# Moving the even heads' outer-key products behind the fourth unit's dense group in a sliding-window attention kernel

## The chip, the cores and the metric

The kernel runs on one core of one Trainium2 chip. The metric is the device time of one execution in microseconds, the median of several runs. A core has five instruction streams that run side by side and wait for one another through semaphores: TensorE (PE; its weight loads are listed apart as PEld), VectorE (DVE), ScalarE (ACT), GpSimd (POOL) and SyncE (SP), which issues the DMAs here. Each stream executes its instructions in the order in which the program lists them, so an instruction that waits holds up everything behind it on its engine.

## The reference

One block of a transformer with conditioned normalization (adaLN): sliding-window attention (32 heads of 16, window 256 over 2048 tokens, 512 features), then a token-mixing MLP (2048 tokens to 1792 and back). Cut to what matters:

```python
def _A_ref(x, wqkv, wo):                      # B, S, D = 1, 2048, 512; H, Dh, W = 32, 16, 256
    q, k, v = ...                             # from x @ wqkv, per head
    scores = jnp.einsum('bhqd,bhkd->bhqk', q, k) * Dh ** (-0.5)
    mask = (idx[:, None] - idx[None, :] >= 0) & (idx[:, None] - idx[None, :] < W)
    p = _softmax(jnp.where(mask[None, None], scores, -1000000000.0), axis=-1)
    o = jnp.einsum('bhqk,bhkd->bhqd', p, v)
    return (lambda x, *d: x.transpose(*d))(o, 0, 2, 1, 3).reshape(B, S, D) @ wo

def _B_ref(x, w1, b1, w2, b2):
    h = _layernorm(x, axis=-1)
    u = _gelu(jnp.einsum('bsd,sf->bdf', h, w1) + b1)
    return (lambda x, *d: x.transpose(*d))(jnp.einsum('bdf,fs->bds', u, w2) + b2, 0, 2, 1)

mod = (_silu(c) @ w_mod).reshape(c.shape[0], 6, 1, -1)      # sa, ca, ga, sb, cb, gb
h = _layernorm(x, axis=-1) * (1 + ca) + sa
x = x + ga * _A_ref(h, A_wqkv, A_wo)
h = _layernorm(x, axis=-1) * (1 + cb) + sb
return x + gb * _B_ref(h, B_w1, B_b1, B_w2, B_b2)
```

## The kernel before

**Tiling of the attention.** The 2048 tokens are four *token groups* (`tg`) of four blocks of 128. The 32 heads are four groups of eight (`g8`), and of the eight, four are even and four odd; the four of one parity sit on the four 32-row strips of TensorE. One *set* is one `tg` with one `g8`: sixteen sets. A set has five *units* `k` (KINDS, L413):

- k = 0 and k = 1: the even heads against the nearer keys, in two parts;
- k = 2: the *outer* keys (the own block's and the far block's half blocks) for even and odd heads together;
- k = 3 and k = 4: the odd heads against the nearer keys.

In the first token group, sets after the first have four units, since k = 0 takes both parities and k = 3 falls away.

For each unit, `emit_scores` (L579) makes the scores in PSUM tiles `pss` (three buffers, two to a unit), `emit_exp` (L646) has ScalarE turn them into `et` with two exponentials of 128x1024 (L659), and the *products* with the values go into the PSUM tile `po`, which has **one** buffer (L417). `av_a` (L664, matmuls on L673) makes a unit's products for the nearer keys; `av_c` (L680, 32 matmuls on L687) those of the outer keys for one parity, with the rearranged values `Vc`. Unit 2's `av_c` completes the even heads, unit 4's `av_a` and `av_c` the odd ones. When a parity is complete, `norm_out` (L716) has VectorE transpose `po` into one half of `t2` (L719); the next parity's products wait for that. After the odd half, `norm_rest` (L724) goes on: the reciprocal `zr` on VectorE (L730), the quotient `merge` on GpSimd (L731), and the transpose into `OTd` on VectorE (L739).

**Dense groups.** Beside the attention's own work, nearly every unit has one *dense group*, sixteen matmuls on L288 into the PSUM tile `dn`, which also has **one** buffer (L418): projections of queries, keys and values (`qk_group` L316, `v_group` L293) for coming sets, the output projection of the token group before (`wo_group` L382), or parts of the MLP's first matmul (`part_group` L806). In two places it is eight transposes (`transpose_group`, L270). VectorE evacuates each group (L304, L330, L333, L397, L822, L278). `plan` (L828) says which group goes to which unit of a token group, `ul` = 5 `g8` + `k`.

**The order.** It is written out by hand (`manual_schedule`). The loop over the units (L977) emits for unit `u`: the first exponential; the scores of unit `u + 1`; then, if `closes` (L997) holds, the products of unit `u - 1`; the dense group; the second exponential; the dense group's evacuation; and, if `closes` does not hold, the products of unit `u - 1` (L1024). `closes` holds where unit `u - 1` completes a parity, that is, where the present unit is k = 3 (after the outer unit 2) or the next set's k = 0 (after unit 4).

```python
            closes = u > 0 and units[u - 1][2] in (2, 4) and u != 3
            if closes:
                products(u - 1)
            group = at.get(ul)
```

**The planner.** The small steps of VectorE (LayerNorm statistics, scalings, `zr`, `OTd`) stand in `chains`, and `fill` (L789) emits them where a hand-kept clock of the engines (`clock`) says that VectorE has room until a given time. `products` (L949) and the loop add estimated costs to this clock and call `fill`, so what stands where in VectorE's queue, and in GpSimd's behind it, hangs on the order of these calls. `ln23` (L742) is the second LayerNorm of a block: statistics (L747, L749), variance and power on GpSimd (L208, L212), VectorE's scaling into `h2` (L759), two products on GpSimd (L763, L764), statistics again, then L208, L212, `shift` (L218) and the final scaling into `hb` (L219) on GpSimd.

**After the attention.** From L1096 on, TensorE runs the MLP's first matmul (L1080) over the blocks `hb` that are ready, with the output projection of the last four blocks in between (`t_wo`, L1099, matmuls on L1102 into `pa`), which needs all four `OTd` of the last token group, the last set's last. Then follow the rest of the first matmul (L1166), GELU (L1091) and the second matmul (L1202). SP loads `w1b` (L1062) and `w2r` (L1064) meanwhile.

Of the kernel before, what the change touches and what calls it, by code (L numbers as in the profile page):

```python
# [30 lines left out]
def kernel(  # L31
# [261 lines left out]
    def v_group(tg, tl, pool, name="dn"):  # L293
        def mms(parts=range(ND), pv=None):
            pv = pv or pool.tile([P, D], DT.float32, name=name)
            for dc in parts:
                dense(
                    pv, lhsT=h1T[tg][:, dc, tl * P : (tl + 1) * P],
                    rhs=wqkv[:, dc, 2 * D : 3 * D], start=(dc == 0), stop=(dc == ND - 1),
                )  # L300
            return pv

        def evac(pv):
            nc.vector.tensor_copy(out=VaugT[tg][:, tl, :, 0:DH], in_=pv[:].rearrange("p (h d) -> p h d", d=DH))  # L304
            if tl > 1:
                nc.vector.tensor_copy(out=Vc[0][0:64, tl, 0:8, :], in_=VaugT[tg][0:64, tl, 0:8, :])
        return mms, evac, 0.9 if tl > 1 else 0.7
# [107 lines left out]
    with tc.manual_schedule():  # L415
# [136 lines left out]
        def k_piece(lo, hi):  # L552
            nc.scalar.activation(out=KT[0][0][:, lo:hi], in_=pk[:, lo:hi], func=ACT.Copy)
# [10 lines left out]
        def both(tg, g8, k):  # L564

            return tg == 0 and g8 > 0 and k == 0

        units = [
            (tg, g8, k) for tg in range(NG) for g8 in range(ND) for k in range(5) if not (both(tg, g8, 0) and k == 3)
        ]  # L570
# [75 lines left out]
        def emit_exp(u, a):  # L646
            tg, g8, k = units[u]
            kind, par, i = KINDS[k]
            n = 512
            if (tg, kind, i) == (0, "A", 0) and not both(tg, g8, k):  # L650

                n = 256
                if a == 0:
                    state["et"] = epool.tile([P, 2, 4 * P], DT.bfloat16, name="et")
                et = state["et"][:, a, :].rearrange("p (h q) -> p h q", h=2)
            else:
                et = (epool if kind == "A" else cpool).tile([P, 2, 4 * P], DT.bfloat16, name="et")
            state["e", tg, g8, k, a] = et
            act = nc.scalar.activation(  # L659
                out=et[:, :, 0:n], in_=state.pop((u, a))[:, :, 0:n], func=ACT.Exp, scale=SCORE_SCALE,  # L660
            )
            return act.ins

        def av_a(tg, g8, k):  # L664
            kind, par, i = KINDS[k]
            if i == 0:
                state["po"] = ps_po.tile([P, 4 * P], DT.float32, name="po")
            merged = i == 0 and both(tg, g8, 0)
            k, shift = (0, 256 * par) if merged else (k, 0)
            for n, (kb, q0, nq, c0) in enumerate(a_pieces(tg, i)):  # L670
                c0 += shift
                for j in range(4):
                    nc.tensor.matmul(  # L673
                        state["po"][32 * j : 32 * j + 32, q0 : q0 + nq],
                        lhsT=VaugT[kb // 4][:, kb % 4, 8 * g8 + 2 * j + par, :],
                        rhs=state["e", tg, g8, k, j // 2][:, j % 2, c0 : c0 + nq],
                        start=(i == 0 and n == 0), stop=False, tile_position=(0, 32 * j), skip_group_check=True,
                    )
# [103 lines left out]
        def add_chain(steps, first=False):  # L782
            chains.insert(0 if first else len(chains), [list(steps), clock["dve"]])
# [5 lines left out]
        def fill(until):  # L789

            while not held[0]:
                for chain in chains:
                    f, cost, *free = chain[0][0]
                    start = max(clock["dve"], chain[1])
                    if start + cost <= until + SLACK + late[0] and start < clock["dve"] + 0.3 and all(x() for x in free):
                        break
                else:
                    break
                chain[0].pop(0)
                clock["dve"] = start + cost  # L800
                given = f()
                chain[1] = on_pool(given) if given else clock["dve"]
                chains[:] = [c for c in chains if c[0]]
# [145 lines left out]
        def products(u):  # L949
            tg, g8, k = units[u]  # L950
            if k in (0, 3):
                clock["pe"] = max(clock["pe"], clock["po"])
            clock["pe"] += (0.34, 0.34, 0.25, 0.34, 0.58)[k]
            if k in (2, 4):
                fill(clock["pe"])
                clock["dve"] = max(clock["dve"], clock["pe"] + 0.05) + 0.73
                clock["po"] = clock["dve"] + 0.1
            if emit_av(u) and k == 4:
                add_chain(norm_rest(tg, g8), first=True)

        def evacuate(group, tile_):
            mms, evac, cost = group
            for_pool = evac(tile_)
            clock["dve"] = max(clock["dve"], clock["pe"] + 0.05) + cost
            clock["dn"] = clock["dve"] + 0.1
            if for_pool:
                on_pool(for_pool)
# [9 lines left out]
        for u, (tg, g8, k) in enumerate(units):  # L977
            ul = u if tg == 0 else 5 * g8 + k
            if ul == 0:
                at, then = plan(tg)  # L980
            half = 0.5 if (tg, g8) == (0, 0) and k in (0, 3) else 0.92
            behind = emit_exp(u, 0)
            if u == 0:
                k_piece(P, 4 * P)
            before = clock["act"]
            clock["act"] = max(clock["act"], ready[u][0]) + half
            if u == 4:
                products(2)
            if u + 1 < len(units):
                emit_scores(u + 1)  # L990
                if units[u + 1][2] == 2:
                    first = max(clock["pe"], before) + 0.3
                    clock["pe"] = max(first, clock["act"] + 0.05) + 0.42
                else:
                    first = clock["pe"] = max(clock["pe"], clock["act"] - 0.1) + 0.4
                ready[u + 1] = (first + 0.1, clock["pe"] + 0.1)
            closes = u > 0 and units[u - 1][2] in (2, 4) and u != 3  # L997
            if closes:
                products(u - 1)
            group = at.get(ul)  # L1000
            held[0] = u in (0, 3)

            late[0] = 0.5 if 4 <= u < 8 else 0.0
            if group:
                tile_ = group[0]()
                clock["pe"] = max(clock["pe"], clock["dn"]) + (0.55 if group[2] > 1 else 0.2 if group[2] == 0.2 else 0.9)
            emit_exp(u, 1)
            clock["act"] = max(clock["act"], ready[u][1]) + half
            if group:
                fill(clock["pe"] + 0.05)  # L1010
                evacuate(group, tile_)
                held[0] = u == 0
                if ul in then:
                    add_chain(then[ul])
            if u == 0:
                mms, evac, cost = v_group(0, 3, ps_s)
                pv = mms(range(ND), ps_s.tile([P, 2, 4 * P], DT.float32, name="pss")[:, 0, :])
                clock["pe"] += 0.9
                evac(pv)
                clock["dve"] = max(clock["dve"], clock["pe"] + 0.05) + cost  # L1020
            elif u == 3:
                products(0)
                products(1)
            elif u > 3 and not closes:  # L1024
                products(u - 1)
            if both(tg, g8, 0) and k == 4:
                clock["pe"] = max(clock["pe"], clock["po"]) + 0.34
                av_a(tg, g8, 3)
            fill(clock["pe"])
            at_unit(tg, ul, u, behind)  # L1030
# [208 lines left out]
```

## Time and profile before

| | |
|---|---|
| median of 3 runs | 259.15 us (258.04 to 259.35) |
| the profiled execution | 258.45 us, its span 256.6 us |
| TensorE busy | 237.3 us (92%) |
| VectorE busy | 170.1 us (66%) |
| ScalarE busy | 160.6 us (63%) |
| GpSimd busy | 126.6 us (49%) |
| 154 exponentials (L659) | 144.1 us, 1018 ns each as listed |

The times in the profile are from the start of the span. A row gives start and length, the engine, the line of the kernel, what is written and read, the shape, and, in brackets, how long the engine stood idle before it and who released it. Lengths of rows that follow each other on one engine overlap: the engine takes up the next instruction before the last has drained, so a step's cost is best read from start to start. The attention stage lasts until about 164 us, the MLP's first matmul until about 205 us, the second until about 253 us. The granted TensorE clock is full throughout.

### The profile page before, as it was taken

What the parts mean: (1) busy time and instruction counts of PE and PEld (TensorE: products, weight loads), DVE (VectorE), ACT (ScalarE), POOL (GpSimd) and SP (SyncE); (2) the same over time, 40 slices, a digit from 0 to 9 for tenths busy, and PEclk for the clock granted to TensorE, in tenths of its full rate; (3) what the DMA queues carried; (4) which work ended last, traced back from release to release, by engine and by line L of the source; (5) the groups of instructions that cost most, each with busy time, mean ns of one, the idle gap of its engine ahead of it and who ended that gap; (6) DMA issues with size and microseconds to landing.
All of it is one profiled execution on the core that took longest, in us unless ns stands there. A gap on an engine that the chain in (4) does not pass through costs nothing.

```text
span 256.6 us, 11298 instructions
## 1 busy us (share of the span) xinstructions
PE 237.3 (92%) x5011; PEld 129.8 (51%) x5011; DVE 170.1 (66%) x360; ACT 160.6 (63%) x187; POOL 126.6 (49%) x216
## 2 busy tenths in 40 slices
PE   6899869998989999989999999999999999999994
PEld 2545435555555556555555555544444444444443
DVE  4759789786798878888778896689603212332544
ACT  6379979999999999999999999400064220000000
POOL 6543973988169998877735698655200000000000
PEclk9999999999999999999999999999999999999999
DMA  6979855145720624200104110699960000202021
GB/s 173 314 249 215 261 133 159 33 90 147 210 86 20 182 62 91 49 17 21 40 20 92 43 25 4 236 411 409 409 259 0 0 0 3 82 0 82 28 97 41
DMA packets 26804, 30.75 MB, mean 120 GB/s; under 512 B 3972, under 2 KB 23428, under 8 KB 26756
## 3 DMA queue, kind: packets, MB, share of 16 engines
q1 hardware_dynamic: 26756, 30.04, 38.4%
q8 instruction: 39, 0.64, 1.0%
q14 instruction: 9, 0.07, 0.1%
HBM read 22.55 MB, written 2.23 MB: 97 GB/s over the span
## 4 chain that ended last, share of the span: by engine, by line
PE 65%; DVE 21%; DMA 4%; ACT 3%; issue 2%; POOL 1%; SPq 1%; DVEq 0%; ACTq 0%
PE py L1202 19%; PE dn L288 18%; PE pu L1080 8%; PE pu L1166 6%; DMA x<-in_A_x_dram 3%; DVE t L719 3%; ACT et L659 3%; PE pss L592 3%; DVE VaugT L304 3%; PE po L673 3%; PE po L687 2%; DVE KT L330 2%; DVE qs L333 2%; DVE x L397 2%; DVE ln_stats L747 2%
## 5 line engine op out<-in xcount | busy, mean ns | idle before, releaser
L659 ACT ACTIVATE et<-pss 128x1024 bf16<-128x1024 f32 (+1 forms) x154 | 144.1, 1018 | 6.8 <-PE pss L609 4.7
L1202 PE MATMUL py<-guT,w2r 128*128 128x512 bf16 (+1 forms) x238 | 48.5, 367 | 0.0
L288 PE MATMUL dn<-h1T,wqkv 128*32 128x512 bf16 (+2 forms) x512 | 33.5, 374 | 3.2 <-DVE qs L333 1.0
L1202 PEld LDWEIGHTS <-w2r 128*128 128x128 bf16 x238 | 23.2, 98 | 25.4
L1181 DVE SCALAR_TENSOR_TENSOR o<-py,bFM,bc 128x512 bf16<-128x512 f32 (+1 forms) x17 | 11.7, 715 | 30.5 <-PE py L1202 30.5
L719 DVE STREAM_TRANSPOSE t<-po 128x512 f32<-128x512 f32 x32 | 22.6, 706 | 7.3 <-PE po L687 7.0
L673 PE MATMUL po<-et,VaugT 128*32 128x64 bf16 (+2 forms) x704 | 24.8, 240 | 2.5 <-DVE t L719 2.5
L212 POOL TENSOR_TENSOR ln_rstd<-ln_ve,mhalf 128x1 f32<-128x1 f32 (+1 forms) x40 | 24.0, 600 | 4.0 <-DVE ln_ve L208 0.7
L592 PE MATMUL pss<-QT,KT 32*128 32x192 bf16 (+2 forms) x704 | 25.1, 237 | 0.4 <-DVE KT L330 0.3
L673 PEld LDWEIGHTS <-VaugT 128*32 128x32 bf16 x704 | 18.2, 96 | 12.6 <-issue 2.5
L208 POOL TENSOR_SCALAR ln_ve<-ln_mv 128x1 f32<-128x1 f32 (+1 forms) x39 | 9.1, 233 | 28.0 <-DVE ln_mv L749 13.9
L288 PEld LDWEIGHTS <-wqkv 128*32 128x32 bf16 x544 | 13.7, 95 | 13.8 <-issue 6.5
L592 PEld LDWEIGHTS <-KT 32*128 32x128 bf16 x704 | 13.7, 92 | 12.8 <-issue 5.7
L731 POOL TENSOR_TENSOR merge<-t,zr 128x512 bf16<-128x512 f32 x16 | 16.9, 1056 | 4.3 <-DVE zr L730 4.3
L1091 ACT ACT_TABLE_LOAD x1 | 1.3, 1283 | 24.7 <-issue 24.7
L609 PE MATMUL pss<-mask_q,mask_k 32*128 32x256 bf16 (+1 forms) x232 | 16.7, 266 | 0.0
L763 POOL TENSOR_TENSOR h<-h,bc 128x512 bf16<-128x512 bf16 x12 | 13.9, 1157 | 4.7 <-DVE h L759 4.7
L1089 DVE TENSOR_TENSOR gelu_a<-pu,part 128x512 f32<-128x512 f32 x8 | 5.2, 686 | 16.4 <-PE pu L1166 16.4
L288 PE MATMUL dn<-wqkv,h1T 128*32 128x512 bf16 x208 | 13.6, 381 | 2.1 <-DVE qs L333 0.8
L764 POOL TENSOR_TENSOR h<-h,bc 128x512 bf16<-128x512 bf16 x12 | 13.9, 1162 | 0.9
L288 PE MATMUL dn<-wod,OTd 128*32 128x512 bf16 x192 | 12.6, 381 | 1.9 <-DVE part L822 0.7
L1166 PE MATMUL pu<-hb,w1b 128*128 128x512 bf16 x64 | 14.3, 379 | 0.0
(120 smaller groups left out, 370.5 us busy)
## 6 DMA issues: line engine op xcount, KB each, us to landing
w2r<-in_B_w_dram SPq DMA_DIRECT2D x14, 512.0 KB, 10.1
w1a<-in_B_w_dram SPq DMA_DIRECT2D x16, 224.0 KB, 2.8
w1b<-in_B_w_dram SPq DMA_DIRECT2D x8, 448.0 KB, 6.5
wmod<-in_w_mod_dram SPq DMA_DIRECT2D x8, 256.0 KB, 3.7
Vc<-VaugT SPq DMA_DIRECT2D x32, 64.0 KB, 3.2
out_dram<-otile SPq DMA_DIRECT2D x15, 128.0 KB, 1.7
x<-in_A_x_dram SPq DMA_DIRECT2D x7, 256.0 KB, 5.9
Vc<-VaugT SPq DMA_DIRECT2D x12, 128.0 KB, 3.5
```

The costliest lines, as they stand in the source:

```text
L212: nc.gpsimd.tensor_tensor(out=r[:], in0=ve[:], in1=mhalf[:, 0:n], op=ALU.pow)
L288: nc.tensor.matmul(out[cols, :], lhsT=lhsT[:, cols], rhs=rhs, start=start, stop=stop, tile_position=(0, 32 * j), skip_group_check=True,)
L592: nc.tensor.matmul(pss[j // 2][:, j % 2, c0 : c0 + nq], lhsT=keys(kb, g8)[rows[j], k0 : k0 + P], rhs=QT[tg][g8][rows[j], p, q0 : q0 + nq], ...
L609: nc.tensor.matmul(pss[j // 2][:, j % 2, :].rearrange("p (a r) -> p a r", a=2)[:, 0:n, :] .rearrange("p a (b q) -> p a b q", q=64)[:, :, 0 ...
L659: act = nc.scalar.activation(out=et[:, :, 0:n], in_=state.pop((u, a))[:, :, 0:n], func=ACT.Exp, scale=SCORE_SCALE,)
L673: nc.tensor.matmul(state["po"][32 * j : 32 * j + 32, q0 : q0 + nq], lhsT=VaugT[kb // 4][:, kb % 4, 8 * g8 + 2 * j + par, :], rhs=state["e" ...
L719: nc.vector.transpose(out=state["t2"][:, par, :], in_=state["po"][:])
L731: nc.gpsimd.tensor_tensor(out=m[:].rearrange("p (b a d) -> p a b d", a=2, d=DH), in0=t2v[:, :, :, 0:DH], in1=zr[:].to_broadcast([P, 2, 16, ...
L763: nc.gpsimd.tensor_tensor(out=h2[:], in0=h2[:], in1=bc_cb1, op=ALU.mult)
L1080: nc.tensor.matmul(pu[:, i, :], lhsT=w1_of(sc, fc), rhs=hb[sc][:], start=(sc == 0), stop=(sc == NT - 1),)
L1166: nc.tensor.matmul(pu[:, i, :], lhsT=w1_of(sc, fc), rhs=hb[sc][:], start=(sc == s0), stop=(sc == NT - 1),)
L1202: nc.tensor.matmul(pys[n][:, 0 : hi - lo], lhsT=w2r[:, fc, tb * P : (tb + 1) * P], rhs=guT[fc][:, lo:hi], start=(fc == 0), stop=(fc == NF ...
```

## The change

One line: `closes` no longer holds where the present unit is k = 3. In the twelve sets of the last three token groups the loop then emits the outer keys' products of the even heads (unit 2's, `av_c` with parity 0) and the transpose of `po` behind the fourth unit's dense group, its second exponential and its evacuation, through the branch at L1024, where they stood ahead of the dense group before. The first token group keeps its order: its first set was already an exception (`u != 3`; there k = 3 is u = 3), and its other sets have no k = 3. Since the planner's clock and its `fill` are called in another order, LayerNorm steps and `OTd` transposes also change places in VectorE's and GpSimd's queues.

```diff
                 ready[u + 1] = (first + 0.1, clock["pe"] + 0.1)
-            closes = u > 0 and units[u - 1][2] in (2, 4) and u != 3
+            closes = u > 0 and k != 3 and units[u - 1][2] in (2, 4)
             if closes:
                 products(u - 1)
             group = at.get(ul)
```

## The prediction

> **Read first.** The busy time by stage (windows over the span) shows which engine limits the attention stage.
>
> ```profile
> core 0: us, PE busy (x) PEld busy (x) DVE busy (x) ACT busy (x) POOL busy (x), PEclk, DMA share, GB/s
> 55.00:95.00 40.00, 36.92 (x1244) 22.75 (x1240) 31.89 (x62) 39.27 (x43) 29.41 (x47) 1.00 0.45 121
> 95.00:135.00 40.00, 36.65 (x1200) 22.13 (x1192) 33.70 (x64) 39.24 (x43) 29.44 (x46) 1.00 0.19 39
> ```
>
> The second number is the window's length, then each engine's busy time. In the stage that the change touches ScalarE's exponentials fill 39.3 of 40 us, TensorE 36.9. So I asked next, for 55 to 170 us, for what ScalarE still waits:
>
> ```profile
> ACT et L659 <- PE pss L609: 1.2, 7, 0.2
> ```
>
> Seven waits, 1.2 us in all. No reordering of TensorE can win more than that here. Then what TensorE waits for, 55 to 165 us:
>
> ```profile
> PE dn L288 <- DVE qs L333: 2.1, 6, 0.5
> PE dn L288 <- DVE part L822: 1.5, 5, 0.4
> PE dn L288 <- DVE KT L330: 1.5, 5, 0.3
> ```
>
> A dense group waits until VectorE has emptied the one buffer `dn`. The timeline of one set around the changed place (TensorE; start, length):
>
> ```profile
> 131.09 1.05 PE L288 MATMUL dn<-h1T,wqkv 128*32 128x512 bf16 x16
> 131.95 0.41 PE L673 MATMUL po<-et,VaugT 128*32 128x256 bf16 x12
> 132.29 0.40 PE L592 MATMUL pss<-QT,KT 32*128 32x256 bf16 x12
> 132.73 0.42 PE L687 MATMUL po<-et,Vc 128*32 128x64 bf16 x32
> 132.97 1.05 PE L288 MATMUL dn<-h1T,wqkv 128*32 128x512 bf16 x16
> 133.95 0.41 PE L592 MATMUL pss<-QT,KT 32*128 32x256 bf16 x12
> 134.81 1.05 PE L288 MATMUL dn<-h1T,wqkv 128*32 128x512 bf16 x16 [0.33 <-DVE qs L333]
> ```
>
> Rows in order: third unit's dense group, products, scores of the fifth unit, **the moved products** (L687, x32), fourth unit's dense group, scores of the next set's first unit, fifth unit's dense group after a wait of 0.33. Last, the end of the attention stage:
>
> ```profile
> 160.98 1.16 POOL L763 TENSOR_TENSOR h<-h,bc 128x512 bf16<-128x512 bf16 x1
> 162.22 1.16 POOL L764 TENSOR_TENSOR h<-h,bc 128x512 bf16<-128x512 bf16 x1
> 165.03 0.35 DVE L730 RECIPROCAL zr<-t 128x32 f32<-128x32 f32 x1
> 165.46 1.05 POOL L731 TENSOR_TENSOR merge<-t,zr 128x512 bf16<-128x512 f32 x1 [2.08 <-DVE zr L730]
> 166.55 0.71 DVE L739 STREAM_TRANSPOSE OTd<-merge 128x512 bf16<-128x512 bf16 x1 [0.40 <-POOL merge L731]
> 166.73 1.89 PE L1102 MATMUL pa<-wod,OTd 128*128 128x512 bf16 x8
> 167.31 0.81 PEld L1102 LDWEIGHTS <-OTd 128*128 128x128 bf16 x5 [0.27 <-DVE OTd L739]
> ```
>
> The last set's quotient goes zr, merge on GpSimd, transpose, output projection `pa`. The fourth weight load of `pa` starts at 167.31, just as the transpose ends (166.55 + 0.71 = 167.26): **no slack**. GpSimd stood idle 2.08 us ahead of that merge. From 164.13 to the end TensorE is the bound (10.00 of 10, 18.00 of 18 us in the windows 172 to 182 and 182 to 200), so whatever delays it here delays the end.
>
> **The change, part by part.** Nothing is added or removed. In twelve sets 32 matmuls (L687), one transpose (L719) and what the planner hangs on them move. ScalarE's and SP's instructions stand in the same order as before; in VectorE's and GpSimd's queues the LayerNorm steps change places.
>
> *Dense groups.* A group's start to the start of its evacuation is 1.09 (132.97 to 134.06, L333), and from there to the next group 0.75 (134.81): pitch at least 1.84. Before, second to third of the rows above took 1.88 (131.09 to 132.97), so without the moved products in front the group can come 0.04 earlier, not 0.24: the products were hiding this wait. Third to fourth is 1.84 before and after. The stall of 0.33 is not saved; about 0.2 of it goes to the fourth unit's dense group. Gain 0.04 x 12 = 0.5 us at most, and only where ScalarE waits. On the other side the next set's scores now come after dense and products: 132.93 + 0.98 + 0.24 = 134.15 for 133.95, **0.20 late**. An exponential follows its scores' start by 0.61 (scores 140.07, exponential 140.68), so it could start at 134.76; ScalarE, at 0.946 apiece (13 in 12.30 us from 140.68) from 131.06, reaches it at 131.06 + 4 x 0.946 = 134.84. Hidden, by 0.08. If that cover is gone, a set loses up to 0.24. Value taken: 0; ends: -1.2 (all of ScalarE's waits) and +2.4 (0.20 x 12).
>
> *The transpose behind the moved products.* It releases the one buffer `po` for the odd heads' products, which stand behind the fifth dense group. Evacuation goes first: 132.93 + 1.09 + 0.61 (an evacuation to the next VectorE start, 134.06 to 134.67) = 134.63, transpose 0.72 to 135.35. TensorE comes to the odd products 0.86 after the fifth dense group's start (131.09 to 131.95): 134.77 + 0.86 = 135.63. Cost 0, cover 0.28; a VectorE step of 0.7 between would cost 0.4. In the new order none stands there but in the last set, where the matmuls end later than that step.
>
> *The last merge on GpSimd.* This is where I put the cost. Before, GpSimd runs after the third set's merge: block 10's four steps (L208, L212, L218, L219), block 11's two products (L763, L764), the **last merge**, block 11's four steps. After, block 11 is ahead: its products come before the third set's merge and its four steps before the last one. Working through GpSimd's new queue in the last group:
> - third set's fourth dense group at 151.99 (before 152.03, less 0.04); evacuation +1.09, next VectorE start +0.61, transpose to next start 0.64 (104.16 to 104.80), then block 10's scaling (L759, 0.37): 154.7;
> - products of blocks 10 and 11: 1.24 + 1.11 + 1.23 + 1.13 (151.43, 152.54, 153.77, 154.90 are such starts) = 4.71, to 159.4;
> - block 9's four steps, 0.30 + 0.66 + 0.37 + 0.73 (155.72, 156.03, 156.69, 157.06, 157.79) = 2.07, to 161.5; merge 1.02 (148.30 to 149.32), to 162.5;
> - block 10's and block 11's four steps, 4.14, to 166.65.
>
> The last merge starts at 166.65, not 165.46: **+1.19**. Transpose and `pa` follow it; no slack, so the end moves by 1.19. Ends: 0 (GpSimd's idle 2.08 takes all of the added 2.07) and +2.07 (none). w2r's loads, which SP issues from 167.40 behind this transpose, come as much later; their first use is at 204.9 us.
>
> *A port shared by two engines.* L759's rows read 0.30 to 0.41 us alone and up to 0.85 beside a GpSimd product; in the new order two L759 stand side by side with block 10's product starting between them. A row's excess, 0.85 - 0.38 = 0.47, is a rival below. The Trainium skill (SBUF — State Buffer, section "SBUF: two separate sides") says that VectorE in a two-port mode and GpSimd take the shared port pair as an exclusive lock and the loser blocks for the whole instruction; by that rule the delay could be an estimated 1.16, a whole product, and the sum 2.35 for 1.19. The trace agrees in kind, not with so long a block.
>
> **Sum:** 0 + 0 + 1.19 on the profiled execution's 258.45 us (span 256.6 and 1.85 around it) = 259.64. The median of the three runs is 259.15, 0.70 above that execution, so the time to expect is 259.15 + 1.19 = **260.3**.
>
> **Rivals.**
> 1. *ScalarE's waits go (not slower).* If fourth and fifth dense groups do close up by the 0.24 that the moved matmuls took, all seven waits vanish: -1.2, against +1.19 at the end, 259.15. For it: the fifth group waits 0.33 in most sets. Against: the pitch of 1.84. It decides if the fourth group starts right behind the scores (132.73).
> 2. *The next set's scores come too late.* 0.20 x 12 = 2.4 on top, 262.7. For it: the cover is 0.08 where ScalarE waits at all. Against: later sets start with more lead, and each of the seven waits swallows some. It decides where exponentials begin to wait at the first unit.
> 3. *VectorE's scaling is blocked by GpSimd* in the last group: +0.47 through the next evacuation, 260.8.
> 4. *The move does nothing and the merge isn't late,* as GpSimd's chain begins over 1.2 us earlier: 259.15.
>
> **Chances.** Forecast 0.48, rivals 0.15, 0.20, 0.08, 0.09. What a measurement tells from no change is 0.5%, 1.3 us; the forecast's 1.19 lies just under it, so I split it 0.22 slower, 0.26 same. Slower: 0.22 + 0.20 + 0.08 = 0.50. Rival 1: 0.10 same, 0.05 faster (if the end costs less than 1.19); rival 4: 0.06 and 0.03. Same 0.42, faster 0.08. Range: below, rival 1 with a third of the end's cost hidden and the runs' own spread, 258.4; above, rival 2 in most of its sets, 262.2. The forecast's own range, ends 0.7 either way, is 259.6 to 261.0.
>
> **What would show it.** Right: the wait for `dn` shows at the fourth and fifth dense groups in like parts; ScalarE's waits stay near 1.2 us; GpSimd's idle 2.08 ahead of the last merge is gone, and TensorE waits about 1.1 us for OTd at L1102. Wrong: a last merge near 165.5, or ScalarE waiting in each set.

## The result, and the profile after

| kernel | median us | runs | ratio to before (95% interval) |
|---|---|---|---|
| before | 258.21 (256.97 to 262.86) | 22 | 1 |
| changed | 260.88 (259.23 to 263.52) | 22 | **1.0099** (1.0075 to 1.0123) |

The change makes the kernel 1.0% slower, 2.6 us (1.9 to 3.2). The profiled execution of the changed kernel took 259.39 us with a span of 257.5; before, 258.45 and 256.6. These two spans differ by 0.9 only, because the changed kernel's execution reached the attention stage about 1 us earlier, ahead of everything that the change touches. So stretches are compared here by their own starts and ends. I took them from the trace's rows of the 154 exponentials (L659), counted in order; the change acts from the 41st on. (Of the runs below, the profiles of the matmuls alone and of block 1's scaling alone are of slow executions; only places and single stretches are read from them.)

| stretch | before, us | after, us | difference |
|---|---|---|---|
| start of the 41st to start of the 101st exponential | 57.70 | 58.52 | +0.82 |
| 101st to 151st | 48.05 | 48.34 | +0.29 |
| 151st to the end of the last | 3.77 | 3.77 | 0 |
| end of the last exponential to the end of the last OTd | 3.74 | 4.70 | +0.96 |
| from there to the end of the span | 89.32 | 89.25 | -0.07 |

That is 2.0 us: half in the attention stage, half in the end that the prediction worked out. The windows that showed the bound before, now of the changed kernel:

```profile
55.00:95.00 40.00, 36.28 (x1189) 22.87 (x1191) 32.08 (x60) 38.60 (x42) 29.18 (x46) 1.00 0.43 118
95.00:135.00 40.00, 36.73 (x1228) 23.21 (x1224) 33.18 (x64) 39.11 (x43) 30.89 (x49) 1.00 0.20 43
```

ScalarE (the fourth figure after the length) falls from 39.27 to 38.60 us in the first window: it stays the bound, but with holes. The waits of the changed kernel, ScalarE's for 55 to 170 us, then TensorE's for 55 to 165:

```profile
ACT et L659 <- PE pss L609: 2.6, 8, 0.7
PE dn L270 <- DVE h1T L278: 1.4, 2, 1.0
PE dn L288 <- DVE KT L330: 0.8, 2, 0.7
PE dn L288 <- DVE part L822: 0.8, 1, 0.8
PE dn L288 <- DVE qs L333: 0.6, 2, 0.3
```

ScalarE waits 2.6 us for scores where it waited 1.2. TensorE's many waits of 0.3 for `dn` have gone (`qs` 2.1 over six before, 0.6 over two now), and a few long ones have come: 1.0 for `h1T`, 0.8 for `part`. The next two timelines show these two places.

**First place, block 1's scaling.** VectorE, GpSimd, TensorE and ScalarE of the changed kernel (start, length, engine and line):

```profile
70.59 0.34 DVE L730 RECIPROCAL zr<-t 128x32 f32<-128x32 f32 x1
71.01 1.20 DVE L759 TENSOR_SCALAR h<-x,ln_mv,ln_rstd 128x512 bf16<-128x512 bf16 x1
72.14 0.98 DVE L278 TENSOR_SCALAR h1T<-dn,modFM 128x512 bf16<-128x512 bf16 x2
71.01 1.06 POOL L731 TENSOR_TENSOR merge<-t,zr 128x512 bf16<-128x512 f32 x1
71.83 0.31 PE L609 MATMUL pss<-mask_q,mask_k 32*128 32x256 bf16 x4
73.18 0.62 PE L270 MATMUL dn<-identity,xn 128*128 128x128 bf16 x8 [1.05 <-DVE h1T L278]
74.67 4.00 ACT L659 ACTIVATE et<-pss 128x1024 bf16<-128x1024 f32 x4 [0.35 <-PE pss L609]
```

The reciprocal `zr` starts GpSimd's merge. In the new order the scaling L759 stands directly behind that reciprocal. It begins at 71.01 as the merge does, and is done 0.15 after the merge (72.07): 1.20 us for work that takes 0.37 alone. Behind it in VectorE's queue stands the evacuation `h1T`, for which the next TensorE group waits 1.05, and ScalarE in turn 0.35. Before, two statistics (L747, L749) stood at that place; the same group waited 0.32, and ScalarE not at all, as the rows of the kernel before show:

```profile
71.79 0.68 DVE L747 BATCH_NORM_STATS2 ln_stats<-x 128x6 f32<-128x512 bf16 x1
72.61 0.96 DVE L278 TENSOR_SCALAR h1T<-dn,modFM 128x512 bf16<-128x512 bf16 x2
73.63 0.62 PE L270 MATMUL dn<-identity,xn 128*128 128x128 bf16 x8 [0.32 <-DVE h1T L278]
64.11 46.51 ACT L659 ACTIVATE et<-pss 128x1024 bf16<-128x1024 f32 x49 [0.16 <-PE pss L609]
```

**Second place, the two scalings of the last group, and the end.** The same kernel, 153 to 169 us:

```profile
153.84 1.75 DVE L759 TENSOR_SCALAR h<-x,ln_mv,ln_rstd 128x512 bf16<-128x512 bf16 x2
157.32 0.63 DVE L822 COPY part<-dn 128x512 f32<-128x512 f32 x1
154.29 1.15 POOL L763 TENSOR_TENSOR h<-h,bc 128x512 bf16<-128x512 bf16 x1
158.00 1.05 PE L288 MATMUL dn<-hb,w1a 128*32 128x512 bf16 x16 [0.77 <-DVE part L822]
159.80 3.77 ACT L659 ACTIVATE et<-pss 128x1024 bf16<-128x1024 f32 x4 [0.67 <-PE pss L609]
...
165.31 0.35 DVE L730 RECIPROCAL zr<-t 128x32 f32<-128x32 f32 x1
165.75 0.77 POOL L219 TENSOR_SCALAR hb<-h,ln_rstd,shift 128x512 bf16<-128x512 bf16 x1
166.48 1.06 POOL L731 TENSOR_TENSOR merge<-t,zr 128x512 bf16<-128x512 f32 x1
167.57 0.71 DVE L739 STREAM_TRANSPOSE OTd<-merge 128x512 bf16<-128x512 bf16 x1 [1.33 <-POOL merge L731]
168.34 1.25 PE L1102 MATMUL pa<-wod,OTd 128*128 128x512 bf16 x5 [0.51 <-DVE OTd L739]
```

Two scalings take 1.75 us: 0.37 for the first, and the second lasts from 154.30 until 0.15 past the end of the product L763 (155.45). Through the evacuation `part` that costs a dense group 0.77 and ScalarE 0.67. The same two rows before had waits of 0.24 and 0.17:

```profile
157.94 1.05 PE L288 MATMUL dn<-hb,w1a 128*32 128x512 bf16 x16 [0.24 <-DVE part L822]
159.75 3.77 ACT L659 ACTIVATE et<-pss 128x1024 bf16<-128x1024 f32 x4 [0.17 <-PE pss L609]
```

The rows of the changed kernel below the "..." show the end: GpSimd works through block 11's steps until 166.5 with no idle time shown, the last merge starts at 166.48 (before: 165.46), the last transpose at 167.57 (before: 166.55), and `pa` waits for it.

### The profile page after: what moved, and what is told of

Read it like the earlier page. It is cut to its first block, busy times and chain, and to the rows that moved or that the text cites. A ratio compares the mean times of both kernels' runs of the same rounds, so it can differ in the third digit from the quotient of the medians.

```text
span 257.5 us, 11300 instructions
## 1 busy us (share of the span) xinstructions
PE 237.4 (92%) x5011; PEld 131.3 (51%) x5011; DVE 170.0 (66%) x360; ACT 160.6 (62%) x187; POOL 127.1 (49%) x216
## 4 chain that ended last, share of the span: by engine, by line
PE 58%; DVE 20%; POOL 8%; DMA 4%; issue 3%; SPq 3%; ACT 3%; ACTq 0%; DVEq 0%
PE py L1202 19%; PE dn L288 16%; PE pu L1080 7%; PE pu L1166 6%; ACT et L659 3%; DVE x L397 2%; DVE qs L333 2%; DVE KT L330 2%; DMA wmod<-in_w_mod_dram 2%; DVE t L719 2%; DVE VaugT L304 2%; PE pss L592 2%; POOL ln_rstd L212 2%; SPq L314 2%; POOL merge L731 2%
## 5 line engine op out<-in xcount | busy, mean ns | idle before, releaser
L659 ACT ACTIVATE et<-pss 128x1024 bf16<-128x1024 f32 (+1 forms) x154 | 144.1, 1017 | 7.4 <-PE pss L609 5.2
L731 POOL TENSOR_TENSOR merge<-t,zr 128x512 bf16<-128x512 f32 x16 | 16.9, 1059 | 6.8 <-DVE zr L730 6.7
L763 POOL TENSOR_TENSOR h<-h,bc 128x512 bf16<-128x512 bf16 x12 | 13.9, 1158 | 3.3 <-DVE h L759 3.3
L288 PE MATMUL dn<-hb,w1a 128*32 128x512 bf16 x208 | 13.6, 381 | 1.3 <-DVE part L822 0.8
L333 DVE CAST qs<-dn 128x512 bf16<-128x512 f32 x15 | 10.3, 687 | 6.4 <-PE dn L288 6.1
L764 POOL TENSOR_TENSOR h<-h,bc 128x512 bf16<-128x512 bf16 x12 | 14.0, 1164 | 0.9
```

Of the source, the lines that this page charges most:

```text
L288: nc.tensor.matmul(out[cols, :], lhsT=lhsT[:, cols], rhs=rhs, start=start, stop=stop, tile_position=(0, 32 * j), skip_group_check=True,)
L333: nc.vector.tensor_copy(out=qs[:], in_=pq[:])
L659: act = nc.scalar.activation(out=et[:, :, 0:n], in_=state.pop((u, a))[:, :, 0:n], func=ACT.Exp, scale=SCORE_SCALE,)
L731: nc.gpsimd.tensor_tensor(out=m[:].rearrange("p (b a d) -> p a b d", a=2, d=DH), in0=t2v[:, :, :, 0:DH], in1=zr[:].to_broadcast([P, 2, 16, ...
```

## The experiments

All ratios are to the kernel before, run in turn on the same chip in five rounds. Single profiles of these runs hold waits of TensorE on nothing that the profile shows (last section); so I read places and stretches in these profiles, not whole spans. A *hole* is a gap between the starts of two exponentials over the usual pitch of 0.946 us; the exponential named is the one after it. The diffs are against the changed kernel, with cuts marked by "...".

**1. The matmuls alone, and the planner alone.** The planner advances its clock for the moved products and fills VectorE's queue by it. In the first run the matmuls and their transpose move while the planner is told of them at the old place; in the second it is the other way round.

```diff
+        def planned():
+            clock["pe"] += 0.25
+            fill(clock["pe"])
+            clock["dve"] = max(clock["dve"], clock["pe"] + 0.05) + 0.73
+            clock["po"] = clock["dve"] + 0.1
...
-            closes = u > 0 and k != 3 and units[u - 1][2] in (2, 4)
-            if closes:
+            closes = u > 0 and units[u - 1][2] in (2, 4) and u != 3
+            moved = closes and k == 3
+            if moved:
+                planned()
+            elif closes:
...
+            elif moved:
+                emit_av(u - 1)
```

(The second run swaps the calls of `planned` and `emit_av`.)

> Moved products and their transpose stand behind the fourth dense group, as in the change, but the planner's clock and fill are called where they were before, so LayerNorm steps keep their places on VectorE and GpSimd. Theory (the planner's new order costs, TensorE's new order nearly nothing): 1.000 to 1.002 of before; ScalarE's waits for scores from 55 us on near 1.2 us, last merge on GpSimd within 0.1 us of zr's end. Rival (TensorE's order costs, the next set's scores 0.2 us late in each set): 1.006 or more, ScalarE's waits 2 us or more.

Measured: 1.0078 (1.0037 to 1.0118). A miss for the theory that I then held, that the planner's order costs and TensorE's nearly nothing; the number is the rival's.

> Products and transpose stay ahead of the fourth dense group, the planner's clock and fill are called as in the change, so LayerNorm steps take their new places. Theory: 1.006 to 1.009 of before, the last merge 1.0 us late and TensorE waiting 0.5 us or more for OTd at the output projection. Rival (TensorE's order costs): 1.004 or less, what the last merge alone costs.

Measured: 1.0240 (1.0174 to 1.0306), far worse than the whole change: both expectations missed. Neither half is a half of the change; each makes a third order, in which TensorE and VectorE do not fit. VectorE and what waits for it in the run with the planner alone:

```profile
149.80 0.72 DVE L719 STREAM_TRANSPOSE t<-po 128x512 f32<-128x512 f32 x1 [0.35 <-PE po L687]
150.44 0.65 DVE L747 BATCH_NORM_STATS2 ln_stats<-x 128x6 f32<-128x512 bf16 x1
151.23 0.66 DVE L822 COPY part<-dn 128x512 f32<-128x512 f32 x1
151.94 1.05 PE L288 MATMUL dn<-wod,OTd 128*32 128x512 bf16 x16 [0.82 <-DVE part L822]
153.75 1.02 ACT L659 ACTIVATE et<-pss 128x1024 bf16<-128x1024 f32 x1 [0.48 <-PE pss L609]
```

The statistics (L747, L749) have slipped ahead of the evacuation L822; TensorE waits 0.82, ScalarE 0.48. Rows of the exponentials show such a hole of 0.4 to 0.7 us in nine sets. In the run with the matmuls alone it is the scaling again:

```profile
155.57 1.14 DVE L759 TENSOR_SCALAR h<-x,ln_mv,ln_rstd 128x512 bf16<-128x512 bf16 x1
156.62 0.68 DVE L822 COPY part<-dn 128x512 f32<-128x512 f32 x1
155.50 1.06 POOL L731 TENSOR_TENSOR merge<-t,zr 128x512 bf16<-128x512 f32 x1
157.36 1.05 PE L288 MATMUL dn<-hb,w1a 128*32 128x512 bf16 x16 [0.85 <-DVE part L822]
159.16 6.52 ACT L659 ACTIVATE et<-pss 128x1024 bf16<-128x1024 f32 x7 [0.58 <-PE pss L609]
```

That hole is 0.68 us, and this run's end (last exponential to last OTd) is 0.22 longer than before's. What the rest of its 2.0 us is, is not shown: the largest hole of this profile, 1.72 at the 79th exponential, stands behind a wait of TensorE on nothing shown.

My reading: what decides is the work that stands ahead of an evacuation in VectorE's queue, and whether it falls beside a long GpSimd instruction. That became the new theory.

**2. The end alone.** Block 11's last statistics are held until the last quotient has been issued.

```diff
+                merged.add((tg, g8))
...
-            return [(p1, 0.8), (p2, 0.37, lambda: len(live) < LIVE), (p3, 0.8)]
+            return [(p1, 0.8), (p2, 0.37, lambda: len(live) < LIVE),
+                    (p3, 0.8, lambda: tb != 11 or (NG - 1, ND - 1) in merged)]
```

> The changed kernel, but block 11's last LayerNorm step is held until the last set's merge has been emitted, as its order was before. Theory: the 1.0 us at the end comes back, 1.005 to 1.007 of before, the last merge starts within 0.1 us of zr and no wait of TensorE for OTd over 0.2 us. Rival (the end's wait is hidden by something later): 1.010, as the change.

Measured: 1.0116 (1.0060 to 1.0172). By its place the edit did what it should:

```profile
157.41 1.76 DVE L760 TENSOR_SCALAR h<-x,ln_mv,ln_rstd 128x512 bf16<-128x512 bf16 x2
169.32 1.06 POOL L731 TENSOR_TENSOR merge<-t,zr 128x512 bf16<-128x512 f32 x1 [1.45 <-DVE zr L730]
```

GpSimd is idle again ahead of the last merge, which begins 0.44 behind its reciprocal, and the stretch from the last exponential to the last OTd is 4.04 us for 4.70. The pair of scalings (here L760) still takes 1.76. By its time the run does not show the 0.7 us: the middle is the rival's (1.010) and not the theory's (1.005 to 1.007). Six runs count, the interval is 2.9 us wide, and the size stays undecided here. The runs of part 4 settle it.

**3. Where in the stage.** The last token group keeps the old order; later, the reverse.

```diff
-            closes = u > 0 and k != 3 and units[u - 1][2] in (2, 4)
+            closes = u > 3 and (k != 3 or tg == NG - 1) and units[u - 1][2] in (2, 4)
```

> The change in the second and third token group alone; the last group keeps the order of before. Theory (the last merge 1.0 us and the blocked scaling of the last group 0.5 us are the bulk): 1.002 to 1.005 of before. Rival (a cost in each of twelve sets alike): two thirds of the change's 2.6 us, 1.0066.

Measured: 1.0037 (0.9988 to 1.0086); the middle lies with the theory, and the interval holds the rival too.

> Only the sets of the last token group have the new order; the two groups ahead are as before. Theory: the pair of scalings in the last group costs 0.5 us and the late last merge 1.0 us, so 1.5 of the 2.0 to 2.4 us are there: ratio to before 1.005 to 1.007; block 1's scaling takes about 0.4 us, block 11's 1.3 us. Rival (the costs lie in TensorE's order, alike in all twelve sets): a third of the change in attention and the last merge, 1.4 us with the end, but block 11's scaling at 0.4 and no wait over 0.3 us at the 151st exponential.

(In the diff `tg < NG - 1` stands for `tg == NG - 1`.) Measured: 1.0052 (1.0016 to 1.0088). Block 11's scaling took 1.30 us, block 1's 0.37, and the hole at the 151st exponential was 0.76. The ratio alone does not decide, since the rival's 1.4 us would be 1.0054; the rows do: the costs sit at places, not in TensorE's order alike in all twelve sets.

**4. The two scalings moved apart.** The decisive runs. TensorE's order stays the changed one in all twelve sets; one scaling may not be issued in the same gap between two evacuations as a quotient or another scaling.

```diff
-                return 1.06
+                beside[0] = emptied[0]; return 1.06
...
-                live.add(tb)
+                live.add(tb); beside[0] = emptied[0]
...
-            return [(p1, 0.8), (p2, 0.37, lambda: len(live) < LIVE), (p3, 0.8)]
+            return [(p1, 0.8), (p2, 0.37, lambda: len(live) < LIVE
+                     and (tb not in (1, 11) or emptied[0] > beside[0])), (p3, 0.8)]
...
-            for_pool = evac(tile_)
+            for_pool = evac(tile_); emptied[0] += cost > 0
```

(`emptied` starts at 1, `beside` at 0; the other runs have `(1,)` or `(11,)` for `(1, 11)`.) On the same chip beside them ran the changed kernel.

> The changed kernel itself, for a measure on the same chip as the three runs beside it. Theory and rival both: 1.010 of the kernel before. In its trace, from the 21st exponential's start to the end of the 154th, 1.1 us more than before's 128.67; from there to the end of the last transpose into OTd 4.7 us (before 3.74); the scaling L759 of block 1 at 1.2 us and of block 11 at 1.3 us.

> One scaling (L759 of block 1) follows the next evacuation instead of the quotient; all else of the changed kernel stays. Theory (that scaling lies beside GpSimd's merge, takes 1.2 us for 0.37, and holds up the evacuation h1T behind it, which costs ScalarE 0.44 + 0.19 us): the two waits at the 62nd and 64th exponential go, attention 0.4 to 0.6 us shorter than the changed kernel's, ratio to before 1.0075 to 1.0085. Rival (the waits come from TensorE's new order alone, VectorE's queue only shows them): the waits stay or move to the next dense group, ratio 1.010.

> The scaling of block 11 no longer stands directly behind that of block 10, but behind the next evacuation that VectorE makes; by this block 11's four small steps on GpSimd also come behind the last merge again. Theory: no wait over 0.3 us at the 151st exponential (0.76 over the pitch in the changed kernel), the last merge starts 0.43 us behind its reciprocal as before, and 1.4 us of the 2.0 are back: ratio to before 1.003 to 1.005. Rival (only GpSimd's end counts, the 151st exponential waits for another reason): 1.0 us back, ratio 1.006, the wait stays.

> The two edits before together; TensorE's order is the changed one in all twelve sets. Theory (the change's cost is VectorE's and GpSimd's new order at three places, not TensorE's): ratio to before 1.000 to 1.003. Rival (TensorE's order costs by itself, in many sets): 1.005 to 1.007.

| kernel | ratio to before (95% interval) | 101st to 151st, us | last exponential to last OTd, us |
|---|---|---|---|
| changed, again | 1.0092 (1.0052 to 1.0132) | 48.31 | 4.67 |
| block 1's scaling later | 1.0044 (1.0004 to 1.0085) | 48.29 | 4.66 |
| block 11's scaling later | 1.0023 (0.9985 to 1.0061) | 47.77 | 3.97 |
| both later | **0.9991** (0.9955 to 1.0027) | 48.28 | 3.97 |

Every matmul of these kernels stands where the change put it. By the middle values each edit gives back a part, block 1's more than I expected (1.0075 to 1.0085); but the interval of either alone overlaps that of the changed kernel. Both together lie clear of it and clear of the rival's 1.005 to 1.007: the time is that of the kernel before. With block 1's scaling behind the evacuations:

```profile
76.18 0.99 DVE L278 TENSOR_SCALAR h1T<-dn,modFM 128x512 bf16<-128x512 bf16 x2
77.91 0.38 DVE L759 TENSOR_SCALAR h<-x,ln_mv,ln_rstd 128x512 bf16<-128x512 bf16 x1
78.33 0.69 DVE L333 CAST qs<-dn 128x512 bf16<-128x512 f32 x1
```

It takes 0.38 for 1.20, and no evacuation is late for it. The holes of the changed kernel at the 63rd, 65th and 75th exponential (0.44, 0.19, 0.18) are gone. With block 11's moved:

```profile
157.97 0.63 DVE L822 COPY part<-dn 128x512 f32<-128x512 f32 x1
159.33 0.76 DVE L759 TENSOR_SCALAR h<-x,ln_mv,ln_rstd 128x512 bf16<-128x512 bf16 x1
166.40 1.05 POOL L731 TENSOR_TENSOR merge<-t,zr 128x512 bf16<-128x512 f32 x1 [0.87 <-DVE zr L730]
157.39 6.84 ACT L659 ACTIVATE et<-pss 128x1024 bf16<-128x1024 f32 x7
```

The last seven exponentials run as one row without a hole, and the last merge waits for its reciprocal, no longer for block 11's steps. The scaling still takes 0.76, beside GpSimd's L219 (159.18 to 159.94), but no evacuation stands directly behind it. (In "both later" 0.50 of the 48.28 is another hole, behind a wait of TensorE on nothing shown; at the 151st exponential its gap is 0.24, as before.)

The first stretch of "changed, again" (58.42 us) can't be set against "both later" (57.88): both hold holes behind waits of TensorE on nothing shown, 0.75 at the 61st exponential in the one and 0.60 at the 79th in the other. Two profiles without such waits can: with block 11's scaling alone moved, block 1's still takes 1.21, the three holes are 0.44, 0.19 and 0.17, and the stretch is 58.29; in the next run, where the matmuls stand alike and both scalings are moved, the holes are gone and it is 57.40.

Whether a scaling is blocked is not fixed by the program alone. In the run of part 2, whose queues here are the changed kernel's, block 1's began 0.16 us ahead of the merge and took 0.32. A third scaling, block 5's, took 0.37 in the first profile of the changed kernel and 1.25 in the second, beside L764. It was blocked for 1.25 to 1.27 in seven profiles, "both later" among them; each of the seven has a hole of 0.36 to 0.40 at the 99th exponential, where the kernel before, the first profile of the changed one and that of the last group alone have 0.10. So a third place of about 0.3 us is probably left in the versions that are level with the kernel before; no run moved this scaling.

**5. A version with the end as before.** Both scalings apart, and in the last set alone the products ahead of the dense group.

```diff
-            closes = u > 0 and k != 3 and units[u - 1][2] in (2, 4)
+            closes = u > 3 and (k != 3 or (tg, g8) == (NG - 1, ND - 1)) and units[u - 1][2] in (2, 4)
```

> The two scalings apart, and in the last set of all the products ahead of the dense group as before. Theory: the end (from the last exponential to the last transpose into OTd) goes from 3.97 back to 3.74 us, attention stays as with both scalings apart: ratio to before 0.997 to 1.000, at best a gain that five rounds hardly tell. Rival (the time of that kernel came from its late end, not from the attention stage): 1.002.

Measured: 1.0018 (0.9985 to 1.0050). Its stretches are 57.40, 47.80 and 3.74 us, together 0.55 less than before's; the end is back at 3.74, as expected. The run's middle is the rival's 1.002, and the interval holds the theory's 0.997 to 1.000 too. The run of part 3 with the last group alone has 57.43 us in the first stretch with the order of before in it, so about half of the 0.55 is scatter between executions. So no version here is shown to be faster than before.

## Why the prediction was right or wrong

**Slower, and the time: right, in part by luck.** 260.3 was forecast within 258.4 to 262.2; the median is 260.88. But the forecast's difference, 1.19 us, was less than half of the measured 2.6; the baseline of three runs (259.15, against 258.21 of 22) was 0.94 too high and hid most of that.

**Dense groups: right.** "Pitch at least 1.84" held: in the changed kernel the fifth group starts 1.84 us behind the fourth in eleven of the twelve sets. The wait came in like parts, as named: 0.13 ahead of the fourth and 0.10 ahead of the fifth group in six sets, where it was 0.00 and 0.33 (0.36 in one). The stall was moved, not saved, and rival 1 (ScalarE's waits go) did not come. One reading was off: where no evacuation stands between two groups, this pitch does not bind. So in the last group's third set the fourth group starts 1.64 behind the third (1.88 before), and in the last set the fifth 1.09 behind the fourth.

**The next set's scores: right.** With both scalings apart and the changed order in all sets, the gap ahead of a set's first exponential is 0.51 over the pitch at the first change of sets (before: 0.26, and 0.19 two exponentials on), 0.10 at one, and at the other nine none above 0.06: the cover of 0.08 all but held. The changed kernel has 0.19 and 0.18 at two more, behind block 1's hole. Rival 2, 0.20 in each set, did not come.

**The last merge: right in its mechanism, too large in its size.** GpSimd's idle 2.08 is gone, and its queue ran as forecast: from the third set's fourth dense group to the last merge 14.98 us (151.50 to 166.48), forecast 14.66, before 13.43. That the merge's time of 166.48 lies so near the forecast 166.65 is luck, since this execution reached the 41st exponential 1.06 us earlier than before's and lost 1.11 from there on. What counts is the reciprocal, which came late too: the merge starts 1.17 behind it for 0.43 before, so GpSimd costs 0.74, not 1.19. TensorE's wait at L1102 shows as 0.51, not about 1.1: part of the delay lies ahead of that row. The stretch to the last OTd is 0.96 longer; experiment 4 returned 0.70 of it by GpSimd's order, and the rest, 0.23 (3.97 less 3.74), is the last set's products standing behind their dense group, which experiment 5 returned.

**The attention stage at 0: wrong, and this is the term that failed.** It was measured at +1.1 (128.67 to 129.79 us from the 21st exponential to the last one's end). The prediction saw that "in VectorE's and GpSimd's queues the LayerNorm steps change places", and then followed these steps in the last group only, and there for their cost on GpSimd. In VectorE's queue their new places ahead of evacuations were the cost: at block 1 in the second token group, which was not looked at, and at the pair in the last one.

**Rival 3 had the mechanism, too cheap and too unlikely.** I had 0.08 for it, and priced a blocked scaling at a row's excess, 0.47. A blocked scaling lasts until just after GpSimd's instruction has ended: 1.20 and 1.29 us, an excess of 0.83 and 0.92, and at two places, not one. The rows for it were in the trace of before: the two that I took for partial slowdowns are scalings that began in the middle. One began at 148.71 beside the merge from 148.30 to 149.35 and ended at 149.50; the other at 150.65 beside L763, 150.19 to 151.35, and ended at 151.50. A length tells only when it began; the ends, 0.15 behind GpSimd's both times, tell the rule. The Trainium skill (SBUF — State Buffer, section "SBUF: two separate sides") says that VectorE in a two-port mode and GpSimd take their shared port pair as an exclusive lock, so that the loser stands still for the whole instruction of the other. I wrote that the trace agrees in kind, not with so long a block; the blocks of 1.20 and 1.29 us beside instructions of 1.06 and 1.15 agree with the page in length too. Which mode these scalings run in, no run here shows. The prediction's estimate by that page, 2.35 in all, came nearer to the measured 2.6 than its sum did, though it was for one place.

Of the signs named, "GpSimd's idle 2.08 gone" and the wait for `dn` in like parts came, and TensorE's wait for OTd in half its size; "ScalarE's waits stay near 1.2 us" failed (2.6), and that failure is the attention stage's 1.1.

## What to carry to other kernels

When a planner or scheduler fills a queue, a moved instruction drags others with it: compare each engine's whole queue before and after, and look at what now stands ahead of every evacuation that another engine waits for. Price a VectorE step of the kind that was held here (a scaling or copy in bf16 that neither reads nor writes PSUM) at the rest of the long GpSimd instruction that it can meet, not at its usual length, and keep such steps behind the evacuations. A "part of the change" made by splitting order from planning is a third order with costs of its own; undoing one consequence at a time, with the change in place, was what told the causes apart.

## What the hardware showed that I had not expected

*A wait to the end of the other engine's instruction.* In the twelve profiles 32 scalings L759 (0.30 to 0.42 us alone) began inside one of GpSimd's merges or products (L731, L763, L764), or up to 0.08 us ahead of it. Of these 29 ended 0.15 us (0.146 to 0.154) after that instruction's end, whatever that made of their length, 0.38 to 1.31 us; the three that began in its last 0.1 us took their usual 0.37. The copies into `Vc` (L306) do the same: 29 that began inside a merge or product, 0.22 alone, ended 0.08 after it, one of 0.94 beside the merge from 52.78 to 53.84 in the changed kernel. VectorE's other rows that began beside such instructions kept their length: between 40 and 164 us of the twelve profiles, evacuations 0.51 to 0.69, statistics 0.65 to 0.69, transposes 0.67 to 0.72, reciprocals 0.34 to 0.36.

It goes the other way too. Of 22 scalings that began inside GpSimd's final scaling L219 (0.77 alone), 11 ended 0.15 after it. The other 11, all but one of which began within 0.03 us of its start, took their usual 0.30 to 0.39, and L219 took 0.87 to 1.00.

*TensorE waiting on nothing shown.* Between the 78th and the 79th exponential ScalarE's gap over the pitch was 0.10, 0.13, 0.14 or 0.23 us in some profiles, 0.47 and 0.60 in two, and 1.42 or 1.72 in four, where TensorE stood 1.1 to 1.4 us in a dense group with its wait put down to "issue". Kernels with the same TensorE order are on both sides. At the 61st exponential even the same kernel is: the changed one has no hole there in its first profile and 0.75 in its second, behind such a wait of 0.78. The cause was not tried. It adds to the scatter of single times.

*The clock ahead of the stage.* In the eight profiles of experiments 1, 2, 4 and the first of 3 the granted clock dipped ahead of the attention stage (0.50 from 30 to 35 us in the run with the matmuls alone, 0.66 from 35 to 40 in that with block 1's scaling) and was 1.00 from 40 us on; in six of them ScalarE's gap between the 22nd and the 23rd exponential was 0.90 to 1.31 us over the pitch, 0.09 otherwise. In the other four profiles the clock was 1.00 in each of these stretches.
